# Half 1's Strassen products ahead of its plain output tile, and two sums of the cross pairs in halves

## The chip, the cores and the metric

The kernel runs on one core of a Trainium2 chip. The metric is the device time of one execution in microseconds; the median over several runs counts. Engines in the profile's names: PE is TensorE's matmuls, PEld its weight loads, DVE is VectorE, ACT is ScalarE, POOL is GpSimd, SP is SyncE, which issues DMAs.

## What is computed

Attention with a local window (96 positions) and a few global keys (8), over 4 batches of 8 heads, 768 positions and head size 64, followed by a gated feed-forward layer on the 3072 x 512 result. Cut to what matters here:

```python
x = attention(q, k, v)                       # 3072 x 512
gate = np.maximum(x @ w_gate, 0.0)           # 3072 x 1536
val  = x @ w_val                             # 3072 x 1536
out  = (gate * val) @ w_out                  # 3072 x 512, float32
```

## The kernel before

**Halves and stages.** The 3072 rows are worked on in eight *halves* c = 0 to 7 (half a batch each, 384 rows, three tiles n of 128 rows). In the steady part, the attention of half c + 1 runs in between the feed-forward work of half c. Halves 0 and 1 share one stage, called stage 1 here: first the gate and value products of both, then the output tiles of both, with the attention of half 2 in between. From half 2 on each half is a stage.

**Feed-forward of a half (`ffn_pieces`).** `f1` holds 24 pieces: for each of 12 column blocks fc a gate product (four matmuls of 384 columns, line 607; ReLU on ScalarE, line 614) and a value product (four matmuls, line 607; the multiplication with the gate on VectorE, line 620, into `ht`). Their results lie in a PSUM pool `ff` of three banks, handed out in turn: a gate takes the bank that the value product two blocks earlier left, a value product the bank of the gate one block earlier. `f2` holds the output pieces. A plain tile (`outp`) is four parts of three matmuls of 512 columns (line 627) into one `ff` bank, a copy on ScalarE (line 632) and a store on SP's queue (line 633).

**Strassen products (`winograd`).** Two output tiles are made together with seven products instead of eight, m1 to m7, six matmuls of 256 columns each (line 549), in an order given as a tuple; in half 1 it is m1, m5, m4, m6, m2, m3, m7. They need four sums of `ht` blocks, s1 to s4 (`add`, line 535, on VectorE, over six blocks or, with two indices, over some of them), and four sums of blocks of the output weights, t1 to t4 (`wo_sum`, line 835, made once, in two parts each, during stage 1). m1 (copy at line 566), m6 (copy at 584) and m7 (additions at 588 and 589) build up in one `ff` bank "a"; m5 (copy at 581) and m3 (addition at 574) in another, "b"; m4 (copy at 578) and m2 (addition at 569) each have a bank of the attention's pool `x`. The copies are ScalarE's, the additions VectorE's. m6 and m7 add onto what is already in bank a, so m7 cannot start before m6's copy has read the bank.

Half 1 has three tiles: n = 0 and 1 as a Strassen pair, n = 2 plain. Halves 4 to 7 have no plain tile: their third tiles are paired across halves (4 with 5, 6 with 7). The seven products of such a cross pair are made in half 5 and half 7; their sums come from `add3`, a second `add`.

**Where the sums stand.** `behind[fc]` lists sums that are issued on VectorE right after the multiplication of block fc (`val_and_sums`). `rest` is the tuple of the sums that need the last blocks; they are inserted between output pieces.

**The order of the work.** The order on each engine is the program's order, written out by hand. `weave` walks through the feed-forward pieces, adds up their weights (0.65 for each) and issues an attention piece, or another placed item, as soon as the walked share of the total reaches the item's place. `spread(items, first, last)` gives a list of items evenly spaced places. So stage 1 reads:

```python
weave(f1_0[G[2]] + f1_1[G[2]] + f2_0 + f2_1,
      [(0.33, order_k[2]), (0.38, order_k[3])],
      spread(attention_pieces(2), 0.375, 0.925), spread(early_pieces(3), 0.58, 0.88),
      spread([... wo_sum(j, part) ... for j in (1, 3, 2, 4) for part in range(2)], 0.1, 0.74))
```

**Attention of a half.** It is made in four pairs of heads, p = 0 to 3. For a pair: scores in two groups of two banks of the pool `x` (line 397), Exp on ScalarE (line 406), masks on VectorE (line 359), then one sum with the values for each of the two heads (line 427, one `x` bank each), Ln and Exp on ScalarE (lines 436, 441), and the normalisation on VectorE into `xT` (line 446), which the next half's gate and value products read. The pool `x` has five banks, handed out in turn in program order to scores, sums, m4 and m2 alike.

Of the kernel before, what the change touches and what calls it, by code (L numbers as in the profile page):

```python
# [15 lines left out]
def kernel(  # L16
# [83 lines left out]
    def w_of(t, dc, fc):  # L100
        f = fc % GW
        return t[fc // GW][:, dc, f * 128 : (f + 1) * 128]
# [495 lines left out]
    def ffn_pieces(c):  # L598
        ht = ht_pool.tile([128, N_FC, QH], BF16, name="ht")
        st = {}  # L600

        def product(w, key, fc, d0, d1):
            key = key, fc
            if d0 == 0 and key not in st:
                st[key] = psum["ff"].tile([128, 512], FP32, name="ff_ps")
            for dc in range(d0, d1):
                nc.tensor.matmul(st[key][:, 0:QH], lhsT=w_of(w, dc, fc), rhs=xT_of[c][:, dc, :],  # L607
                                 start=(dc == 0), stop=(dc == N_DC - 1))

        def gate(fc, d0=0):  # L610
            product(wg, "g", fc, d0, N_DC)
            psg = st["g", fc]
            gr = gr_pool.tile([128, QH], BF16, name="grelu")
            nc.scalar.activation(gr, psg[:, 0:QH], AF.Relu, bias=0.0, scale=1.0)  # L614
            st["gr", fc] = gr

        def val(fc, d0=0):
            product(wv, "v", fc, d0, N_DC)
            psv = st["v", fc]
            nc.vector.tensor_tensor(ht[:, fc, :], psv[:, 0:QH], st["gr", fc], op=ALU.mult)  # L620

        def outp(n, part):
            if part == 0:
                st["o"] = psum["ff"].tile([128, 512], FP32, name="ff_ps")
            ps2 = st["o"]
            for fc in range(part * N_FC // 4, (part + 1) * N_FC // 4):
                nc.tensor.matmul(ps2, lhsT=ht[:, fc, n * 128 : (n + 1) * 128],  # L627
                                 rhs=wo_sb[:, fc, :],
                                 start=(fc == 0), stop=(fc == N_FC - 1))
            if part == 3:  # L630
                osb = late["osb"].tile([128, DM], FP32, name="osb")
                nc.scalar.copy(osb, ps2)
                nc.sync.dma_start(out=out_v[c, n], in_=osb)

        def begin():
            two = psum["s"].tile([128, 2, 512], FP32, name="s_ps")
            st["g", 1], st["v", 1] = two[:, 0], two[:, 1]
            for d0, d1 in ((0, 2), (2, N_DC - 1)):
                for key, w in (("g", wg), ("v", wv)):
                    for fc in range(2):  # L640
                        product(w, key, fc, d0, d1)

        plain = range(NN) if c < 1 else () if c - c % 2 in PAIRED else (NN - 1,)
        add, products = winograd([(c, ht, 0), (c, ht, 1)], "sums", (1, 5, 6, 4, 7, 2, 3) if c == NHALF - 1 else
                                 (1, 2, 5, 6, 4, 3, 7) if c in PAIRED else (1, 5, 4, 6, 2, 3, 7))
        behind = {2: [lambda: add(3, 0, 3)], 7 if c == 2 else 5: [lambda: add(3, 3, 6)], 8: [lambda: add(1, 0, 3)],
                  9: [lambda: add(2, 0, 3)], 10: [lambda: add(4, 0, 3)]}
        rest = tuple(lambda j=j: add(j, 3, 6) for j in (1, 2, 4))
        if c in PAIRED:
            third_of[c] = ht  # L650
        elif c - 1 in PAIRED:
            add3, products3 = winograd([(c, ht, NN - 1), (c - 1, third_of[c - 1], NN - 1)], "sums3",
                                       (1, 5, 4, 6, 2, 3, 7))
            behind.update({1: [lambda: add3(1)], 6: [lambda: add3(2)], 7: [lambda: add3(3)]})
            rest = (lambda: add3(4),) + rest

        def val_and_sums(fc):
            val(fc)
            for f in behind.get(fc, ()):
                f()  # L660

        begin_of[c] = (begin, lambda fc=0: gate(fc, N_DC - 1), lambda fc=0: val(fc, N_DC - 1))
        f1 = []
        for fc in range(N_FC):
            f1.append((0.65, lambda fc=fc: gate(fc)))
            f1.append((0.65, lambda fc=fc: (val if c < 1 else val_and_sums)(fc)))
        f2 = [(0.65, lambda n=n, part=part: outp(n, part))
              for n in plain for part in range(4)]
        if c >= 1:
            f2 += (products3 if c - 1 in PAIRED else []) + products  # L670
            places = (2, 3, 5) if plain else (0, 1, 2) if c in PAIRED else (0, 1, 2, 3)
            for at, f in list(zip(places, rest))[::-1]:
                f2.insert(at, (0.0, f))
        return f1, f2


    def spread(items, first, last):

        n = len(items)
        return [(first + (i + 0.5) / n * (last - first), f) for i, (_, f) in enumerate(items)]  # L680
# [100 lines left out]

    stack = open_psum(ff=2, s=2, t=2)
    f1_0, f2_0 = ffn_pieces(0)
    f1_1, f2_1 = ffn_pieces(1)
    g_of = [lambda fc=fc: begin_of[0][1](fc) for fc in range(2)] + [f for _, f in f1_0[4::2]]
    v_of = [lambda fc=fc: begin_of[0][2](fc) for fc in range(2)] + [f for _, f in f1_0[5::2]]
# [18 lines left out]
    for f in ("m0 g0 g1 v0 m3 K3 m2 g2 m1 v1 K2 v2 S30 K0 S31 K1 S21 g3 S20 v3 S01 A3 N3 S00 S11 "  # L805
              "g6 g7 A2 S10 g4 v7 A0 N2 v4 v6 A1 N0 N1 g5 v5").split():
        i = int(f[1])
# [20 lines left out]
    def wo_sum(j, part):  # L828
        n2 = N_FC // 2
        i = slice(part * n2 // 2, (part + 1) * n2 // 2)  # L830
        b = lambda upper, cols: wo_sb[:, upper * n2 : (upper + 1) * n2][:, i, cols]
        t = {k: late["t"][k][:, i] for k in late["t"]}
        x, y, op = {1: (b(0, c1), b(0, c0), ALU.subtract), 2: (t[3], b(0, c0), ALU.add),
                    3: (b(1, c1), b(0, c1), ALU.subtract), 4: (t[2], b(1, c0), ALU.subtract)}[j]
        nc.vector.tensor_tensor(t[j], x, y, op=op)
# [9 lines left out]
    for f in (*casts[:7], lambda: nc.gpsimd.tensor_copy(held, wo_sb[0:1, N_FC - 1, 0:1]),  # L845
# [7 lines left out]
          [(0.33, order_k[2]), (0.38, order_k[3])],  # L853
          spread(attention_pieces(2), 0.375, 0.925), spread(early_pieces(3), 0.58, 0.88),
          spread([(0.0, lambda j=j, part=part: wo_sum(j, part)) for j in (1, 3, 2, 4) for part in range(2)],
                 0.1, 0.74))

    ahead = {}
    for c in range(2, NHALF):
        placed = []  # L860
        if c + 2 < NHALF:
            load_qk(c + 2, 0, H)
            load_v_half(c + 2)
            placed.append(spread(early_pieces(c + 2), 0.25, 0.75))
        if c + 1 < NHALF:
            pieces = ahead.pop(c + 1, None) or attention_pieces(c + 1)
            if c in PAIRED:

                placed.append([(0.76, pieces[-2][1]), (0.84, pieces[-1][1])])
                placed.append(spread(pieces[:-2], 0.05, 0.7))  # L870
            else:
                placed.append(spread(pieces, *(0.07, 0.82) if c == 2 else (0.0, 0.8)))
        if c + 1 in PAIRED:
            ahead[c + 2] = attention_pieces(c + 2)
            placed.append(spread([ahead[c + 2].pop(0) for _ in range(3)], *(0.885, 0.975) if c - 1 in PAIRED else (0.82, 0.93)))
        f1, f2 = ffn_pieces(c)
        weave(f1 + f2, *placed)
# [35 lines left out]
```

## Time and profile before

| | |
|---|---|
| median of 3 runs | 239.83 us (239.14 to 240.46) |
| time of the profiled execution | 240.08 us |
| its span on the core | 238.3 us |
| TensorE matmuls busy | 231.7 us (97%), 1977 of them |
| VectorE busy | 171.8 us (72%) |
| ScalarE busy | 156.1 us (66%) |
| GpSimd busy | 89.5 us (38%) |

The profile is of one execution; its rows give start and duration of groups of instructions. A row of TensorE's timeline merges neighbouring matmuls of one kind, and the drawn end of a matmul is a model: groups that follow each other without a wait overlap in the drawing. Starts are therefore compared with starts. Stage 1's output tiles run from about 57 to 76 us, half 2's gate and value products begin at about 76 us, and half 5 runs from about 156 to 185 us. TensorE's listed waits over the whole span add up to 2.9 us, 1.3 of it the first one.

### The profile page before, as it was taken

The numbers are of one execution on the slowest core, as the hardware profiler recorded it, in microseconds if no ns is written. First come the engines' busy times: TensorE is split into PE (matmuls) and PEld (weight loads), VectorE is DVE, ScalarE is ACT, GpSimd is POOL, SyncE is SP. The second block draws the span as 40 slices with busy tenths as digits, with TensorE's granted clock in tenths as the row PEclk, the third lists the DMA queues.
The fourth block names the chain that finished last, engine by engine and source line by source line (L and its number), as shares of the span: only waits on it lengthen the run. The fifth ranks groups of instructions, "written<-read, shape, count | busy, mean of one in ns | idle before, by whom it ended". The sixth has DMA issues, their size and how long they took to land.

```text
span 238.3 us, 5431 instructions
## 1 busy us (share of the span) xinstructions
PE 231.7 (97%) x1977; PEld 150.1 (63%) x1981; DVE 171.8 (72%) x456; ACT 156.1 (66%) x358; POOL 89.5 (38%) x204
## 2 busy tenths in 40 slices
PE   7899999999999999999999999999999999999994
PEld 3655565655557566666667666856588666766683
DVE  7775965768756778666787677868985786955752
ACT  5896983438767777757777678557686578634330
POOL 6795897007433860903275042723350000000000
PEclk9999999999999999999999999999999999999999
DMA  6999999993996897098519955198432200020022
GB/s 208 183 170 174 241 263 213 191 162 47 286 205 124 260 194 135 10 183 259 101 33 111 236 155 111 25 157 249 78 59 88 90 1 0 4 88 0 3 80 97
DMA packets 70515, 31.42 MB, mean 132 GB/s; under 512 B 47176, under 2 KB 67400, under 8 KB 70488
## 3 DMA queue, kind: packets, MB, share of 16 engines
q0 software_dynamic: 32800, 8.71, 36.0%
q1 hardware_dynamic: 36472, 21.45, 34.3%
q10 hardware_dynamic: 1216, 0.92, 1.2%
q8 instruction: 15, 0.25, 0.4%
q14 instruction: 12, 0.10, 0.1%
HBM read 28.41 MB, written 6.29 MB: 146 GB/s over the span
## 4 chain that ended last, share of the span: by engine, by line
PE 86%; DMA 7%; DVE 2%; POOL 1%; ACT 1%; issue 1%; DVEq 0%
PE ff_ps L607 50%; PE ff_ps L549 12%; DMA wg<-in_moe_w_gate_dram 7%; PE ff_ps L627 7%; PE x_ps L427 6%; PE x_ps L549 5%; PE x_ps L397 4%; PE t_ps L700 1%; PE t_ps L459 1%; POOL kq L737 1%; PE t_ps L272 1%; DVE es L359 0%; DVE ht L620 0%; ACT lnd L436 0%; DVE osb L574 0%
## 5 line engine op out<-in xcount | busy, mean ns | idle before, releaser
L607 PE MATMUL ff_ps<-xT,wg 128*128 128x384 bf16 x380 | 77.7, 326 | 0.4 <-DMA wg<-in_moe_w_gate_dram 0.2
L607 PE MATMUL ff_ps<-xT,wv 128*128 128x384 bf16 x380 | 77.6, 326 | 0.2 <-DVE osb L574 0.2
L614 ACT ACTIVATE grelu<-ff_ps 128x384 bf16<-128x384 f32 x95 | 46.5, 491 | 45.1 <-PE ff_ps L607 23.2
L620 DVE TENSOR_TENSOR ht<-ff_ps,grelu 128x384 bf16<-128x384 f32 x95 | 52.7, 555 | 30.2 <-PE ff_ps L607 19.1
L607 PEld LDWEIGHTS <-wg 128*128 128x128 bf16 x384 | 36.1, 98 | 23.6 <-issue 1.0
L607 PEld LDWEIGHTS <-wv 128*128 128x128 bf16 x384 | 35.8, 98 | 23.3 <-issue 0.5
L406 ACT ACTIVATE es<-x_ps 128x360 bf16<-128x360 f32 (+2 forms) x96 | 35.6, 447 | 3.2 <-PE x_ps L397 3.2
L359 DVE TENSOR_TENSOR es<-es,m_all 128x432 bf16<-128x432 bf16 (+4 forms) x108 | 29.7, 325 | 6.0 <-ACT es L406 5.8
L446 DVE TENSOR_TENSOR xT<-x_ps,rcp 64x384 bf16<-64x384 f32 x48 | 26.6, 554 | 9.2 <-ACT rcp L441 8.4
L436 ACT ACTIVATE lnd<-x_ps 64x384 f32<-64x384 f32 x48 | 23.3, 485 | 10.9 <-PE x_ps L427 10.2
L363 POOL CAST kqc<-ks 128x384 bf16<-128x384 f32 x24 | 12.1, 554 | 31.7 <-DMA ks<-in_k_dram 31.7
L549 PEld LDWEIGHTS <-s 128*128 128x128 bf16 x216 | 21.1, 98 | 2.9 <-issue 0.4
L549 PE MATMUL ff_ps<-t,s 128*128 128x256 bf16 x162 | 21.6, 272 | 0.3 <-ACT osb L584 0.3
L427 PE MATMUL x_ps<-es,vbuf 128*128 128x216 bf16 (+4 forms) x216 | 21.8, 225 | 0.0
L137 POOL DMA_DIRECT2D vbuf<-in_v_dram x25 | 21.6, 881 | 0.3 <-DVE s L535 0.3
L427 PEld LDWEIGHTS <-vbuf 128*128 128x128 bf16 x216 | 15.8, 97 | 6.8
L627 PE MATMUL ff_ps<-wo_sb,ht 128*128 128x512 bf16 x68 | 17.6, 379 | 0.2
L549 PEld LDWEIGHTS <-ht 128*128 128x128 bf16 x162 | 15.5, 98 | 2.3
L263 POOL COPY kT<-kqT 128x240 bf16<-128x240 bf16 x16 | 7.1, 442 | 22.2 <-DMA kqT<-kqc 19.2
L363 POOL CAST kqc<-qs 128x384 bf16<-128x384 f32 x24 | 12.1, 541 | 6.2 <-DMA qs<-in_q_dram 6.2
L535 DVE TENSOR_TENSOR s<-ht 128x384 bf16<-128x384 bf16 (+1 forms) x32 | 12.5, 392 | 0.8
L441 ACT ACTIVATE rcp<-lnd 128x384 f32<-128x384 f32 x24 | 12.6, 524 | 0.8
(118 smaller groups left out, 247.0 us busy)
## 6 DMA issues: line engine op xcount, KB each, us to landing
out_dram<-osb SPq DMA_DIRECT2D x23, 256.0 KB, 2.4
ks<-in_k_dram SPq DMA_DIRECT2D x6, 768.0 KB, 6.2
qs<-in_q_dram SPq DMA_DIRECT2D x6, 768.0 KB, 11.5
vbuf<-in_v_dram POOLq DMA_DIRECT2D x21, 120.0 KB, 7.7
wo_sb<-in_moe_w_out_dram POOLq DMA_DIRECT2D x1, 1536.0 KB, 19.0
wg<-in_moe_w_gate_dram POOLq DMA_DIRECT2D x2, 512.0 KB, 9.8
wv<-in_moe_w_val_dram POOLq DMA_DIRECT2D x2, 512.0 KB, 11.0
wg<-in_moe_w_gate_dram POOLq DMA_DIRECT2D x2, 256.0 KB, 5.8
```

Of the source, the lines that this page charges most:

```text
L137: nc.gpsimd.dma_start(out=v_dst(b, NG + r0, NG + r0 + n, j), in_=v[b, :, KT * j + r0 : KT * j + r0 + n, :].rearrange("h p d -> p h d"))
L359: nc.vector.tensor_mul(for_all, for_all, mk)
L363: nc.gpsimd.tensor_copy(kqc[:, :, i].rearrange("t n (h d) -> t h n d", d=D)[:, 2 * p : 2 * p + 2], of[s][:, 2 * p : 2 * p + 2, :].rearrang ...
L406: nc.scalar.activation(es[:, e, 0:c], banks[e][:, 0:c], AF.Exp, bias=0.0, scale=scale)
L427: nc.tensor.matmul(av3[:, :, a : a + w], lhsT=vb[:, j, z0 : z0 + 128], rhs=es[:, e, c : c + NN * w].rearrange("k (n p) -> k n p", n=NN), s ...
L436: nc.scalar.activation(ln[o0 : o0 + 64], av[d0 : d0 + 64, 0:QH], AF.Ln, bias=0.0, scale=1.0)
L446: nc.vector.tensor_tensor(xT_of[s][r, p, :], av_of[s, p, e][r, 0:QH], av_of[s, p, "r"][r], op=ALU.mult)
L549: nc.tensor.matmul(st[key][:, 0:D2], lhsT=left(i), rhs=right(i), start=start and i == 0, stop=i == N2 - 1, skip_group_check=not start)
L607: nc.tensor.matmul(st[key][:, 0:QH], lhsT=w_of(w, dc, fc), rhs=xT_of[c][:, dc, :], start=(dc == 0), stop=(dc == N_DC - 1))
L614: nc.scalar.activation(gr, psg[:, 0:QH], AF.Relu, bias=0.0, scale=1.0)
L620: nc.vector.tensor_tensor(ht[:, fc, :], psv[:, 0:QH], st["gr", fc], op=ALU.mult)
L627: nc.tensor.matmul(ps2, lhsT=ht[:, fc, n * 128 : (n + 1) * 128], rhs=wo_sb[:, fc, :], start=(fc == 0), stop=(fc == N_FC - 1))
```

## The change

Three things are changed.

1. Half 1's seven Strassen products come ahead of its plain tile. Before, the plain tile's four parts came first and the products ended the stage; now the four parts of the plain tile (its quarters) do. The three sums in `rest` (second halves of s1, s2 and s4), which stood between the pieces of half 1's own outputs, are inserted into half 0's output pieces, at places 3, 6 and 9 of its list.
2. The sums s2 and s3 of the cross pairs (halves 5 and 7) are issued in two operations of three blocks each instead of one of six: s2 behind value blocks 3 and 6, s3 behind 4 and 7, where they stood whole behind 6 and 7.
3. The weight sums t1 to t4 are spread over 0.1 to 0.66 of stage 1 instead of 0.1 to 0.74.

```diff
@@ -651,7 +651,9 @@
         elif c - 1 in PAIRED:
             add3, products3 = winograd([(c, ht, NN - 1), (c - 1, third_of[c - 1], NN - 1)], "sums3",
                                        (1, 5, 4, 6, 2, 3, 7))
-            behind.update({1: [lambda: add3(1)], 6: [lambda: add3(2)], 7: [lambda: add3(3)]})
+            behind[1] = [lambda: add3(1)]
+            for fc, j, i in ((3, 2, 0), (4, 3, 0), (6, 2, 3), (7, 3, 3)):
+                behind[fc] = [lambda j=j, i=i: add3(j, i, i + 3)]
             rest = (lambda: add3(4),) + rest
 
         def val_and_sums(fc):
@@ -666,7 +668,12 @@
             f1.append((0.65, lambda fc=fc: (val if c < 1 else val_and_sums)(fc)))
         f2 = [(0.65, lambda n=n, part=part: outp(n, part))
               for n in plain for part in range(4)]
-        if c >= 1:
+        if c == 1:
+
+            f2 = products + f2
+            for at, f in zip((3, 6, 9), rest):
+                f2_0.insert(at, (0.0, f))
+        elif c > 1:
             f2 += (products3 if c - 1 in PAIRED else []) + products
             places = (2, 3, 5) if plain else (0, 1, 2) if c in PAIRED else (0, 1, 2, 3)
             for at, f in list(zip(places, rest))[::-1]:
@@ -853,7 +860,7 @@
           [(0.33, order_k[2]), (0.38, order_k[3])],
           spread(attention_pieces(2), 0.375, 0.925), spread(early_pieces(3), 0.58, 0.88),
           spread([(0.0, lambda j=j, part=part: wo_sum(j, part)) for j in (1, 3, 2, 4) for part in range(2)],
-                 0.1, 0.74))
+                 0.1, 0.66))
```

On TensorE and ScalarE the number of instructions stays the same; VectorE gets four more.

## The prediction

> **What bounds the kernel now.** I read the page's busy times first, then TensorE's waits, then the timelines of TensorE, ScalarE and VectorE around the places where TensorE waits.
>
> ```profile
> PE 231.7 (97%) x1977; PEld 150.1 (63%) x1981; DVE 171.8 (72%) x456; ACT 156.1 (66%) x358; POOL 89.5 (38%) x204
> ...
> PEclk9999999999999999999999999999999999999999
> ```
>
> TensorE is busy 231.7 of 238.3 us at full granted clock. A faster VectorE or ScalarE is worth only what TensorE waits for them.
>
> ```profile
> PE ff_ps L549 <- ACT osb L584: 0.3, 1, 0.3
> PE ff_ps L607 <- DVE osb L574: 0.2, 1, 0.2
> PE ff_ps L607 <- DVE ht L620: 0.2, 1, 0.2
> ```
>
> These are all the waits that the change can touch (the others are start-up). The first two end stage 1, the third is in half 5. The rows give their true size:
>
> ```profile
> 73.87 0.82 PE L549 MATMUL x_ps<-wo_sb,ht 128*128 128x256 bf16 x6
> 74.53 0.82 PE L549 MATMUL ff_ps<-wo_sb,s 128*128 128x256 bf16 x6
> 75.60 0.81 PE L549 MATMUL ff_ps<-t,s 128*128 128x256 bf16 x6 [0.26 <-ACT osb L584]
> 76.25 0.81 PE L607 MATMUL ff_ps<-xT,wg 128*128 128x384 bf16 x4
> 77.31 0.81 PE L607 MATMUL ff_ps<-xT,wv 128*128 128x384 bf16 x4 [0.24 <-DVE osb L574]
> ```
>
> Undisturbed groups start 0.65 us apart (73.87 to 74.53), though each is drawn 0.82 long. m7 starts 1.07 after m3: it lost 0.42. Half 2's first value product starts 1.06 after its gate product: it lost 0.41. A wait's cost here is its listed idle time plus 0.16.
>
> ```profile
> 70.52 0.59 ACT L632 COPY osb<-ff_ps 128x512 f32<-128x512 f32 x1 [0.16 <-PE ff_ps L627]
> 71.01 0.84 ACT L406 ACTIVATE es<-x_ps 128x360 bf16<-128x360 f32 x2
> ...
> 74.77 0.52 ACT L441 ACTIVATE rcp<-lnd 128x384 f32<-128x384 f32 x1
> 75.20 0.35 ACT L584 COPY osb<-ff_ps 128x256 f32<-128x256 f32 x1
> ```
>
> m6, started at 73.22, had ended at 74.03, but its copy (L584) stood behind the attention's Ln and Exp on ScalarE until 75.20; m7 adds onto the bank that this copy reads. In the same way L574 stood behind the last normalisations on VectorE (until 76.52) and held the bank of half 2's value product.
>
> ```profile
> 169.27 0.81 PE L607 MATMUL ff_ps<-xT,wv 128*128 128x384 bf16 x4
> ...
> 170.26 0.81 PE L607 MATMUL ff_ps<-xT,wg 128*128 128x384 bf16 x4 [0.17 <-DVE ht L620]
> ```
>
> ```profile
> 167.04 0.56 DVE L620 TENSOR_TENSOR ht<-ff_ps,grelu 128x384 bf16<-128x384 f32 x1 [0.37 <-PE ff_ps L607]
> 167.52 0.71 DVE L535 TENSOR_TENSOR s<-s,ht 128x768 bf16<-128x768 bf16 x1
> 168.15 1.59 DVE L359 TENSOR_TENSOR es<-es,m_all 128x432 bf16<-128x432 bf16 x4
> 169.66 0.55 DVE L620 TENSOR_TENSOR ht<-ff_ps,grelu 128x384 bf16<-128x384 f32 x1
> ```
>
> In half 5, gate 9 takes the bank that value 7 leaves (three banks in turn); value 7's multiplication waits behind a 768-wide sum and four masks. Gate 9 starts 0.99 after value 8 instead of 0.65: 0.34 lost. All three losses make 1.17 us: the most that can be won.
>
> **Part 1: stage 1's order.** No work is added or taken away; I lay out the new order with the old rows. Up to 66.33 nothing on TensorE changes. Then three matmuls end half 0's last tile (0.65); m1 at 66.98, m5 at 67.64 (its copy is now at once behind m1's on ScalarE), pair 3's scores from 68.3 with their switch (0.47 together), m4 due at 68.77.
>
> The five x banks go round: pair 2's scores X0 to X3, pair 1's sums X4 and X0, pair 3's scores X1 to X4. Next before came pair 2's sums (X0, X1), m4 (X2), pair 3's sums (X3, X4), m2 (X0). Now it is m4 (X0), pair 2's sums (X1, X2), m2 (X3), pair 3's sums (X4, X0). Two waits are new:
> - m4's X0 is free when pair 1's second normalisation ends, 68.74; with the 0.05 between a release and a start (L584's end 75.55, m7 75.60) m4 starts at 68.79: 0.02 lost.
> - m2's X3 holds pair 3's scores of the second group until their Exp has run. That Exp now stands on ScalarE behind m6's copy, and m6's copy behind m6. Pair 2's first sum is at 69.44, m6 at 69.72, the second sum at 70.37, so m2 is due at 70.65. m6 ends 0.81 after its start, 70.53; its copy starts at 70.58. L632 above lasts 0.59 and the next activation starts 0.49 after it, 0.10 before its end; so after a copy of 0.35 the Exp starts at 70.83, and one of the 360-wide ones lasts 0.48: 71.31. m2 starts at 71.36: **0.71 lost**. Behind that Exp wait only its twin and pair 2's second Ln.
>
> The old waits go. m7 comes at 72.67, long after m6's copy (70.93). Half 2's value product takes the bank of m7, whose additions end by 75.4, before 77. What is late next: pair 3's sums at 73.33 (VectorE makes m2's addition 72.22 to 72.65, then two masks to 73.17: in time), the plain tile's 12 matmuls from 73.94 (2.6), gate 0 at 76.54, value 0 at 77.19 against 77.31 before. Gate 0's fourth matmul needs pair 3's normalisation: Ln, Ln, Exp end about 75.3, the normalisations 76.5, needed at 77.08. Sum: -0.83 + 0.73 = **-0.10 us**. Bounds of the new waits: 0 (the bank is free in time) to 1.1 (m2 needs the twin Exp too, 0.36 later); I take 0.73, since every row in it is measured at this shape.
>
> Edits at nothing: the three second-half sums move into half 0's output tiles (0.35 each, 1.05 in all) under 1.37 us in which VectorE idles before 62.68, waiting for an Exp. Without that cover, pair 2's scores at 63.45 would wait for pair 0's normalisation, by up to 1.05 less 0.2 of slack. The wo sums (0.74 to 0.66) come at most 2 us earlier; t4's second half then ends about 65.9 instead of 69.33, before m4. On SP the plain tile's store is now last, issued near 77.4 instead of 77.9 for m7's, so half 4's loads behind it are no later. POOL's queue is the same.
>
> **Part 2: sums in halves.** A 768-wide sum takes 0.55 (546 ns mean), a 384-wide one 0.35, and the next starts about 0.08 before its end. Each split adds some 0.12 to 0.15 us of VectorE, four times. In half 7 TensorE never waits, so it costs nothing. In half 5 the first halves go behind values 3 and 4: at 163.1, in 0.83 us of idle time, and at 164.5, where they push pair 2's normalisations and value 5 (165.72) by 0.17; gate 7 takes that bank at 166.50, and is due at 166.77. Behind value 6 there is 0.27 less work, more at the stretched pace (0.71 for 0.55) that this stretch shows. The masks' inputs are ready by 167.6, so value 7 starts 0.27 to 0.36 earlier, and gate 9 loses 0.07 to 0 instead of 0.34: **-0.29 us**. Bounds: -0.34 to +0.1.
>
> The stretch has a cause in the rows: while POOL's casts run (166.86 to 169.2), the sum takes 0.71 for 0.55, the first two masks 0.68 and 0.48 for 0.37 and 0.18, and two casts 0.83 and 0.65 for 0.51. The new half-sum at 164.5 meets the four casts from 164.55; that is rival 3 below. The Trainium skill, SBUF — State Buffer, Who interferes with whom, says that a VectorE instruction with two SBUF inputs and a GpSimd one that reads SBUF exclude each other, the later one waiting out the earlier. The stretched rows agree. Perfetto Trace Analysis, Optimizing Scalar/DVE Operations, in the Trainium skill puts some 60 ns of access overhead on each VectorE operation on SBUF and advises larger ones when the engine is saturated, smaller ones when it is not but makes others wait. By its first half the four splits would be an estimated 0.24 us of loss.
>
> **Sum.** Against the profiled execution (240.08; span 238.3 and 1.8 around it): -0.10 - 0.29 = -0.39, 239.69. That execution is 0.25 above the median of 239.83, so a median of 239.44: **239.4**.
>
> **Rivals.**
> 1. No new wait: X3 is free when m2 comes. Then all 1.17 comes back: 238.7. For it: every old wait does go. Against: m6's copy stands ahead of that Exp, and m6 ends only 0.12 before m2 is due.
> 2. Slower: half 2's start becomes bound by pair 3's normalisation. m2's addition now stands on VectorE ahead of pair 3's last masks, and m7's two additions (0.75) ahead of pair 3's normalisations. I left 0.58 us. Before, sums to end of normalisation took 3.91 (72.56 to 76.47). If that holds and the 0.75 comes on top, 4.66 stands against 3.75 to gate 0's fourth matmul: 0.91 lost. With no gain in half 5: -0.83 + 0.73 + 0.91 = +0.81, 240.6; with the masks at the stretched pace (1.59 for 0.98) +1.4. It decides once the chain takes over 3.75. Against: ScalarE's copies that lengthened it before are gone from it.
> 3. The change doesn't do what it says in half 5: the half-sum at 164.5 waits out a cast (0.51). Value 5 ends near 167.0, gate 7 starts at 167.05 for 166.77, 0.28 lost, and the win at gate 9 is spent. Left is -0.10: 239.7.
>
> **How the numbers follow.** Forecast 0.50, rival 1 0.15, rival 2 0.20, rival 3 0.15. A difference under 0.5% (1.2 us) is about what a measurement of this kernel can't tell from none; the runs themselves spread over 1.3. The forecast and rival 3 are "same" but for 0.03 on each side by that spread; rival 1, at 1.17, falls over the line half the time (0.07); rival 2, between 0.8 and 1.4, half the time (0.10). Faster 0.10, same 0.77, slower 0.13. The range runs from rival 1 with little spread, 238.6, to rival 2's first price, 240.6.
>
> **What would show it.** Right: no wait at m7 or half 2's value 0; a wait of about 0.55 listed (0.71 start to start) at m2, L549 x_ps, released by ACT es L406; half 2's gate 0 at about 76.5; none or under 0.1 at gate 9. Wrong: a listed wait for DVE xT L446 at half 2's start (rival 2), no wait at m2 (rival 1), one at half 5's gate 7 (rival 3), or any new wait before 66 us.

## The result and the profile after

The changed kernel takes 238.91 us (median of 22 runs, 238.27 to 240.08) against 239.74 for the kernel before in the same sessions (22 runs): ratio 0.9965, interval 0.9953 to 0.9978, so 0.83 us less, between 0.53 and 1.13. The forecast was 239.4, or 0.39 less. Its profiled execution took 238.84 us with a span of 237.0.

TensorE's timeline at the end of stage 1 (start, duration, line, tiles, count):

```profile
66.16 0.81 PE L627 MATMUL ff_ps<-wo_sb,ht 128*128 128x512 bf16 x3
...
70.22 0.44 PE L427 MATMUL x_ps<-es,vbuf 128*128 128x216 bf16 x4
70.50 0.82 PE L549 MATMUL x_ps<-wo_sb,ht 128*128 128x256 bf16 x6
71.15 0.82 PE L549 MATMUL ff_ps<-wo_sb,s 128*128 128x256 bf16 x6
71.81 0.82 PE L549 MATMUL ff_ps<-t,s 128*128 128x256 bf16 x6
72.46 0.71 PE L427 MATMUL x_ps<-es,vbuf 128*128 128x216 bf16 x8
73.01 2.75 PE L627 MATMUL ff_ps<-wo_sb,ht 128*128 128x512 bf16 x12
75.60 0.81 PE L607 MATMUL ff_ps<-xT,wg 128*128 128x384 bf16 x4
76.25 0.81 PE L607 MATMUL ff_ps<-xT,wv 128*128 128x384 bf16 x4
```

No row has a wait. m7 (71.81) follows m3 by 0.66 and half 2's value product follows its gate by 0.65: the two old waits are gone. m2 (70.50) follows pair 2's second sum at once: the new wait of 0.71 us, on which the forecast's wash rested, is not there. From the first of these rows to the last it is 10.09 us; the same two points lie 10.98 apart before (66.33 to 77.31). Stage 1 gives **0.89 us**.

ScalarE's rows around m2 are where the forecast had them, once its times are moved by the 0.17 us that this execution was ahead at 66.16:

```profile
70.42 0.37 ACT L584 COPY osb<-ff_ps 128x256 f32<-128x256 f32 x1
70.69 0.84 ACT L406 ACTIVATE es<-x_ps 128x360 bf16<-128x360 f32 x2
```

m6's copy was forecast for 70.41 and the Exp for 70.66. So m2 started before the Exp that should have freed its bank: it was given another bank.

In half 5, gate 9 follows value 8 by 0.82 us, against 0.99 before and 0.65 undisturbed:

```profile
168.20 0.81 PE L607 MATMUL ff_ps<-xT,wv 128*128 128x384 bf16 x4
169.02 0.81 PE L607 MATMUL ff_ps<-xT,wg 128*128 128x384 bf16 x4
```

That is 0.17 us. The rest of the 1.3 us between the two spans is 0.17 that this execution was already ahead before 28 us, where the change touches nothing, and less than 0.1 elsewhere.

Two theories had to be told apart. **Theory A**: stage 1's new order gives the 0.89, and half 5's 0.17 comes from the halved sums. **Theory B**: half 5's wait depends on when POOL's casts of q run beside VectorE's masks, and the halved sums have little to do with it. And two rivals for stage 1: the order of the products, or VectorE's sums having been moved up.

### The profile page after: what moved, and what is told of

The parts are those of the page before. It is cut to its first block, busy times and chain, and to the rows that moved or that the text cites. A ratio compares the mean times of both kernels' runs of the same rounds, so it can differ in the third digit from the quotient of the medians.

```text
span 237.0 us, 5436 instructions
## 1 busy us (share of the span) xinstructions
PE 231.0 (97%) x1981; PEld 149.5 (63%) x1981; DVE 171.5 (72%) x460; ACT 156.4 (66%) x358; POOL 88.7 (37%) x204
## 4 chain that ended last, share of the span: by engine, by line
PE 87%; DMA 9%; POOL 1%; DVE 1%; issue 0%; SPq 0%
PE ff_ps L607 52%; PE ff_ps L549 12%; DMA wg<-in_moe_w_gate_dram 7%; PE ff_ps L627 7%; PE x_ps L427 6%; PE x_ps L549 5%; PE x_ps L397 4%; DMA kq<-in_k_dram 2%; PE t_ps L459 1%; POOL kq L744 1%; PE s_ps L459 0%; POOL wv L155 0%; POOL wg L155 0%; DVE qk L281 0%; SPq L182 0%
## 5 line engine op out<-in xcount | busy, mean ns | idle before, releaser
L359 DVE TENSOR_TENSOR es<-es,m_all 128x432 bf16<-128x432 bf16 (+4 forms) x108 | 28.6, 316 | 5.1 <-ACT es L406 5.0
L535 DVE TENSOR_TENSOR s<-ht 128x384 bf16<-128x384 bf16 (+1 forms) x34 | 13.1, 386 | 0.8
```

The source lines that it names most:

```text
L359: nc.vector.tensor_mul(for_all, for_all, mk)
```

## The experiments

Each code cut is the edit against the changed kernel, where nothing else is said. Stage 1's length below is from the start of the last three matmuls of half 0's third tile to the start of half 2's first value product.

**Stage 1's edits alone: the order, the moved sums and the earlier weight sums** (called "order alone" below)

```diff
-            behind[1] = [lambda: add3(1)]
-            for fc, j, i in ((3, 2, 0), (4, 3, 0), (6, 2, 3), (7, 3, 3)):
-                behind[fc] = [lambda j=j, i=i: add3(j, i, i + 3)]
+            behind.update({1: [lambda: add3(1)], 6: [lambda: add3(2)], 7: [lambda: add3(3)]})
```

> Half 1's order and the earlier weight sums alone, the cross pairs' sums whole. Theory (stage 1 gives the larger part, because both old waits go and m2's bank is free): from the last three matmuls of half 0's third tile to half 2's first value product 10.1 us as in the changed kernel, against 10.98 before; half 5's gate 9 starts 0.99 us after value 8 as before. In all 0.9 us less than before, ratio 0.996. Rival (the halved sums carry the gain, stage 1 is the wash that the prediction had): ratio 0.999.

Measured: 238.75 us, ratio 0.9964 (0.9948 to 0.9981), the whole gain of the change. Stage 1 takes 10.09 us (66.20 to 76.29). The expectation for half 5 was wrong: with the sums whole, gate 9 waits for nothing.

```profile
168.24 0.81 PE L607 MATMUL ff_ps<-xT,wv 128*128 128x384 bf16 x4
168.89 0.81 PE L607 MATMUL ff_ps<-xT,wg 128*128 128x384 bf16 x4
```

This is the same instruction order in half 5 as before, and 0.34 us less of a wait. Theory A's second half falls: 0.34 us can go without any halved sum.

**The halves alone**

```diff
-            behind.update({1: [lambda: add3(1)], 6: [lambda: add3(2)], 7: [lambda: add3(3)]})
+            behind[1] = [lambda: add3(1)]
+            for fc, j, i in ((3, 2, 0), (4, 3, 0), (6, 2, 3), (7, 3, 3)):
+                behind[fc] = [lambda j=j, i=i: add3(j, i, i + 3)]
```

(the edit against the kernel before)

> The cross pairs' sums in halves alone, stage 1 as before. Theory: stage 1 10.98 us with both waits; gate 9 0.82 us after value 8, as in the changed kernel, 0.17 us won, ratio 0.9993. Rival (the halves carry the gain): 0.6 us or more won, ratio 0.9975 or less.

Measured: 239.49 us, ratio 1.0000 (0.9987 to 1.0013). Stage 1 takes 10.97 us with both waits; gate 9 starts 0.64 after value 8, not the expected 0.82. The halves alone move nothing that can be measured.

**The plain tile first, all else as changed**

```diff
-            f2 = products + f2
+            f2 = f2 + products
```

> The changed kernel, but with half 1's plain tile ahead of its products again; the sums moved into half 0's tiles, the weight sums up to 0.66 and the halved sums stay. Theory (the order of the products carries stage 1's gain): m7 waits 0.42 us start to start for m6's copy and half 2's first value product 0.41 for VectorE, as before; only half 5's 0.17 us are won, ratio 0.9993. Rival (VectorE was late because the sums and weight sums stood among its last pieces): both waits at least halve, stage 1 10.5 us or less, ratio 0.997.

Measured: 239.67 us, ratio 1.0003 (0.9988 to 1.0017). Stage 1 takes 10.97 us, with both waits back:

```profile
76.23 0.81 PE L549 MATMUL ff_ps<-t,s 128*128 128x256 bf16 x6 [0.25 <-ACT osb L584]
76.89 0.81 PE L607 MATMUL ff_ps<-xT,wg 128*128 128x384 bf16 x4
77.93 0.81 PE L607 MATMUL ff_ps<-xT,wv 128*128 128x384 bf16 x4 [0.23 <-DVE osb L574]
```

So without the order of the products nothing is won; moving the sums and the weight sums up brings nothing by itself.

**m2 in the bank that the prediction gave it**

```diff
             V2(r(0, 0), block("c", raw(0, 1), of_b(1, c0)), r(0, 0), op=ALU.add)
+            if pair[0][0] == 1:
+                nc.vector.tensor_copy(rc_pool.tile([1, 1], BF16, name="held2"), st["d"][0:1, 0:1])
```

> The changed kernel, with m4's bank kept by a one-element copy on VectorE after m2's addition, so that m2 gets the bank of pair 3's second group of scores, the one that the prediction gave it. Theory (the prediction's price was right and only the bank wrong): m2 waits 0.55 us as listed, 0.7 start to start, for ACT es L406; stage 1 10.8 us; 0.7 us slower than the changed kernel, ratio to before 0.9985. Rival (the price was wrong too, the Exp comes in time): no wait at m2, ratio 0.9955.

Measured: 239.47 us, ratio 0.9992 (0.9975 to 1.0010). Stage 1 takes 10.81 us (65.97 to 76.78), and m2 waits as it was forecast to:

```profile
70.03 0.43 PE L427 MATMUL x_ps<-es,vbuf 128*128 128x216 bf16 x4
71.03 0.81 PE L549 MATMUL x_ps<-wo_sb,ht 128*128 128x256 bf16 x6 [0.56 <-ACT es L406]
```

It starts 1.00 after the second sum instead of 0.28: 0.72 us, against the 0.71 of the prediction's working. The price was right; the bank was not. The built programs, in which every tile has its bank, show why. The banks of pool `x` are not handed out in turn, as the description ahead of the prediction has it: each new tile gets the bank whose last reader comes first in the program. For stage 1's tiles of the kernel before, both rules give the same banks, so that order could not tell them apart. In the changed kernel m4's copy, which frees m4's bank, stands ahead of the Exps of pair 3's second group, and m4 and m2 have one and the same bank. It was free from 69.87 (69.50 + 0.37) on:

```profile
69.50 0.37 ACT L578 COPY osb<-x_ps 128x256 f32<-128x256 f32 x1 [0.27 <-PE x_ps L549]
```

In this run a late reader keeps m4's bank, and m2 has the bank that the group's first Exp frees.

**The weight sums as late as before**

```diff
-                 0.1, 0.66))
+                 0.1, 0.74))
```

> The changed kernel with the weight sums spread to 0.74 again. On VectorE the second half of t4 then stands behind pair 1's normalisations, which end 0.1 us before m4 is due. Theory (the earlier weight sums are needed by the new order): m4 starts about 0.5 us late, a wait of some 0.35 us listed there for DVE t; ratio to before 0.9975. Rival (they are not needed): stage 1 10.1 us, no new wait, ratio 0.9955.

Measured: 238.93 us, ratio 0.9964 (0.9936 to 0.9991), too wide to tell 0.25 us. In the profile stage 1 takes 10.32 us: the fourth matmul of m4 starts about 0.25 late (at 69.80), since the half of t4 that it needs ends only at 69.75 (69.19 + 0.56). The first three matmuls need the other half, which the expectation of 0.5 forgot. So in this one profile the shift to 0.66 is worth about a quarter of a microsecond to the new order; the times neither confirm nor deny it.

**Half 5: other places for the sums or the casts**

```diff
-            for fc, j, i in ((3, 2, 0), (4, 3, 0), (6, 2, 3), (7, 3, 3)):
-                behind[fc] = [lambda j=j, i=i: add3(j, i, i + 3)]
+            for fc, j, i in ((3, 2, 0), (3, 3, 0), (7, 2, 3), (8, 3, 3)):
+                behind[fc] = behind.get(fc, []) + [lambda j=j, i=i: add3(j, i, i + 3)]
```

> The changed kernel with the cross pairs' half-sums in other places: both first halves behind value 3, the second halves behind 7 and 8, so that none stands between value 6 and the masks. Theory (value 7 is late by what stands ahead of it on VectorE): gate 9 starts 0.65 us after value 8, 0.17 us less than the changed kernel, ratio to before 0.995. Rival (the work is only pushed on): another gate or value product of half 5 waits by 0.1 us or more, nothing won.

```diff
-            placed.append(spread(early_pieces(c + 2), 0.25, 0.75))
+            placed.append(spread(early_pieces(c + 2), *(0.45, 0.85) if c == 5 else (0.25, 0.75)))
```

> The changed kernel with half 7's casts on POOL, which run in half 5 while the sums and masks do, spread from 0.45 to 0.85 of that half instead of 0.25 to 0.75. Theory (what is left of gate 9's delay comes from VectorE's operations stretching beside POOL's casts): the half-sums ahead of value 7 take 0.35 us instead of 0.6, the four masks 0.98 instead of 1.28, gate 9 starts 0.65 us after value 8; 0.17 us less than the changed kernel, ratio 0.995. Rival (VectorE's queue is too long there in any case): gate 9 still 0.75 us or more after value 8.

Measured: 238.69 us, ratio 0.9952 (0.9926 to 0.9977), and 238.53 us, ratio 0.9940 (0.9916 to 0.9964). Gate 9 follows value 8 by 0.65 in both. But so it did in the run with whole sums, so neither tells what it was meant to tell; nor do their times, whose intervals overlap that of the changed kernel (0.9953 to 0.9978). The second one did not even move the casts: POOL's casts of q still started when the load of q had landed, which was 0.34 us before value 6 started on TensorE.

That number is what orders the profiles. "Casts" is the start of the four casts of q on POOL less the start of value 6 on TensorE; "gate 9" is its start less that of value 8.

| kernel | sums | casts | gate 9 |
|---|---|---|---|
| before | whole | +0.75 | 0.99 |
| changed, first profile | halves | +0.52 | 0.82 |
| order alone | whole | -0.09 | 0.65 |
| m2's bank | halves | -0.19 | 0.64 |
| halves alone | halves | -0.38 | 0.64 |
| plain tile first | halves | -0.59 | 0.64 |
| weight sums at 0.74 | halves | -0.71 | 0.65 |

In this table only the two profiles with a late start of the casts have a late gate 9, whatever the sums.

**The casts held back.** To set this start by the program instead of leaving it to the load, a one-element copy on POOL, which reads value 6's block, was put ahead of the four casts, with the sums whole, in halves, and in the other places:

```diff
             val(fc)
+            if c == 5 and fc == 7:
+                nc.gpsimd.tensor_copy(rc_pool.tile([1, 1], BF16, name="gate"), ht[0:1, 6, 0:1])
```

> Half 1's new order with the cross pairs' sums whole, and the four casts of half 7's q on POOL held until value 6 of half 5 is multiplied, by a one-element copy ahead of them. Theory (gate 9's wait comes from these casts running beside VectorE's sum and masks, and so from when the q load lands): masks stretch to 1.3 us or more together, value 7's multiplication is late, gate 9 starts 0.85 to 1.05 us after value 8 instead of 0.65. Rival (the wait has another cause): 0.65 as in the run with the order alone.

> The changed kernel (sums in halves) with the same held casts. Theory (halving takes 0.27 us from what stands ahead of value 7, which only shows when the casts are late): gate 9 starts 0.2 to 0.3 us earlier than with whole sums, 0.65 to 0.8 after value 8. Rival (halving brings nothing even then, since a half-sum waits out a cast as a whole one does): the same as with whole sums within 0.1 us.

> The half-sums in other places (both first halves behind value 3, the second ones behind 7 and 8) with the same held casts. Theory: no sum stands between value 6 and the masks, value 7 is another 0.3 us earlier, gate 9 starts 0.65 us after value 8. Rival (the casts meet the masks whatever stands ahead of them): 0.75 or more.

With whole sums, VectorE's, POOL's and TensorE's rows read:

```profile
166.48 0.55 DVE L535 TENSOR_TENSOR s<-s,ht 128x768 bf16<-128x768 bf16 x1
166.95 2.75 DVE L359 TENSOR_TENSOR es<-es,m_all 128x432 bf16<-128x432 bf16 x4
169.62 0.55 DVE L620 TENSOR_TENSOR ht<-ff_ps,grelu 128x384 bf16<-128x384 f32 x1
```

```profile
167.02 1.83 POOL L363 CAST kqc<-qs 128x384 bf16<-128x384 f32 x4
```

```profile
168.23 0.81 PE L607 MATMUL ff_ps<-xT,wv 128*128 128x384 bf16 x4
170.22 0.81 PE L607 MATMUL ff_ps<-xT,wg 128*128 128x384 bf16 x4 [1.17 <-DVE ht L620]
```

The four masks take 2.75 us instead of 0.98; gate 9 follows value 8 by 1.99. With halves it is 1.76 (168.16 to 169.92), with the sums elsewhere 1.52 (168.38 to 169.90). One run each: 240.02, 239.73 and 239.72 us, with 239.45 for the kernel before. The masks stretched to 2.75 in all three, far beyond the expected 1.3, so the absolute numbers missed, and in the third run the rival's number (0.75 or more) came true. The hold put the casts 1.75 to 1.95 us after value 6's start, later than any load did (0.75 at most), so these runs show the cause and not the size of the wait before. The steps between them (0.23 and 0.24) are what moving a half-sum away from ahead of the masks is worth in that case, from one profile each. Theory B holds: the wait is the casts', and the halves shorten it only when the casts are late.

**The casts past the masks, and the changed kernel again**

```diff
             val(fc)
+            if c == 5 and fc == 7:
+                nc.gpsimd.tensor_copy(rc_pool.tile([1, 1], BF16, name="gate"), ht[0:1, 7, 0:1])
```

> The changed kernel with half 5's q casts held until value 7 is multiplied, past the masks. Theory (casts cost only where they meet masks ahead of a product that TensorE waits for): the four masks take 0.98 us, gate 9 starts 0.65 us after value 8 in any run, and no later product of half 5 waits; as fast as the changed kernel's best executions, up to 0.2 us below its median, ratio to before 0.9955. Rival (the collision only moves): gate 10 or a later product waits by 0.2 us or more, ratio 0.997 or above.

> The changed kernel itself once more, beside the run with the held casts. Theory: stage 1 10.1 us as in its first profile; gate 9 between 0.65 and 0.85 us after value 8, by how late the q casts begin after value 6 starts on TensorE (0.17 us lost for 0.52, nothing for a start before it). Rival (halving the sums fixed what gate 9 loses): always 0.82.

Measured: 238.65 us, ratio 0.9961 (0.9943 to 0.9979), and 238.74 us, ratio 0.9961 (0.9943 to 0.9980). With the casts held until value 7 the masks take 0.98 and gate 9 comes at 0.65; no other product of half 5 waits. The changed kernel's second profile has its casts 0.64 before value 6, and gate 9 at 0.65 as well, with the same code as in its first profile, where it was 0.82. POOL's rows of the two, the first profile's first:

```profile
165.56 2.10 POOL L363 CAST kqc<-qs 128x384 bf16<-128x384 f32 x4 [0.32 <-DMA qs<-in_q_dram]
```

```profile
163.85 1.98 POOL L363 CAST kqc<-qs 128x384 bf16<-128x384 f32 x4 [0.23 <-DMA qs<-in_q_dram]
```

Value 6 started at 165.04 and at 164.49, and both times the casts had waited for the load of q. In these medians nothing is left to be won by holding the casts.

## Why the prediction was right or wrong

**What bounds the kernel: right.** The only listed waits that could be won were those three, and the difference between the two profiles lies there and at the start. The loss per wait, listed idle time plus 0.16, held within 0.01 in every run (0.56 listed and 0.72 lost at m2). One row was misread without harm: before, the last normalisations on VectorE ended at 76.47 (75.33 + 1.14), not 76.52, and m2's addition stood between them and L574; the loss of 0.41 is as stated.

**The old waits of stage 1 go: right**, both, and the run with the plain tile first shows that they stay without the new order. The term (0.83) was a little small: m6 also waited 0.11 before, for m1's copy behind ScalarE's Ln and Exp (L566, 72.81 to 73.16). That is too short to be listed; it shows when pair 3's two sums to the next product (72.56 to 73.22, 0.66) are compared with the 0.55 that they take now.

**m2's new wait of 0.71: wrong.** The step that failed is "the five x banks go round". Every duration in its sum came out within 0.03 us, but the bank was another one. What the runs showed in its place is that m2 gets the bank that m4's copy has freed, and waits for nothing; given the other bank, it does lose the 0.72. No wait at m2 is the prediction's own sign of being wrong, and rival 1 came true for stage 1: 0.89 won instead of 0.10. m4's wait for its bank was there, about 0.05 instead of 0.02.

**Half 5's 0.29: wrong as a gain of the change.** The row of 1.59 us of masks beside POOL's casts was read rightly as a stretch, but the stretch was taken as a property of the kernel rather than of the one execution. Whether the casts run then depends on when q's load lands. In the changed kernel's first profile gate 9 still lost 0.17, in its second nothing, and the halves alone give a ratio of 1.0000. Two of its sums were off too. Halving takes 0.20 us from behind value 6 (0.55 less 0.35), not 0.27; the held runs show 0.21 on VectorE from value 6's multiplication to value 7's (3.62 and 3.41). And with the next operation starting 0.08 before the end, a split adds 0.07 (twice 0.27 for 0.47), not 0.12 to 0.15. How often the kernel before has its wait is not known: there is one profile of it. Adding 0.89 for stage 1 and nothing for half 5 agrees with the measured 0.83 (0.53 to 1.13).

**That the time came near the forecast is in part luck.** 239.4 was forecast, within 238.6 to 240.6, and 238.91 measured, but neither term held: stage 1 gave 0.79 more than its 0.10, half 5 none of its 0.29. The second error hid a part of the first, and 0.44 was left between the two medians' differences (0.83 and 0.39).

**Rivals 2 and 3** did not occur. Half 2's first gate product needs pair 3's normalisation, which ended at 75.66 (74.52 + 1.14), 0.4 before its fourth matmul started (75.60 + 0.49). The half-sum at 163.37 did meet a cast (0.60 for 0.35), but gate 7 came on time (165.71, 0.67 after value 6).

**The edits at nothing** cost nothing: before 66 us TensorE has no new wait. The shift of the weight sums, entered as no cost, carries a part of the gain: without it m4 lost about 0.25 in the one profile taken.

## What to carry to other kernels

When a wait's price hangs on which buffer of a pool an operation gets, look up the buffer in the built program before pricing it; here the place of the last reader in the program decided, not the number of the request. A stall that one profile shows beside a transfer's landing time is to be taken as chance until a second profile, or a run that holds the transfer, shows it again. Where TensorE is the bound, work that needs the other engines only at its very end (here a plain tile, with one copy) can fill the time behind work whose results must pass through busy engines on the way (here the products that build up in shared banks); in this kernel that order was worth 0.89 us.

## What the runs showed of the hardware

By the drawn rows, one VectorE mask was held out by four POOL casts in a row. In the run with whole sums and held casts, the first mask alone, two SBUF inputs of 432 elements, took 2145 ns, from 166.95 to 169.10; the other mask of this size in the same run took 0.37 us. Meanwhile the four casts ran undisturbed from 167.02 to 168.85; the mask's drawn start is even 0.07 before the first cast's. The view of line 359 in that stretch (duration min/median/max):

```profile
L359 DVE TENSOR_TENSOR es<-es,m_all x4: 169/332/2145, 166.9 to 169.4; 128x432 bf16<-128x432 bf16 x2, 128x48 bf16<-128x48 bf16 x1, 128x288 bf16<-128x288 bf16 x1
```

The other two held runs show the same: 2149 ns for the first mask with the halved sums, and with the sums elsewhere 1946 ns for the second mask, of 48 elements, which takes 0.17 us otherwise.

The Trainium skill, SBUF — State Buffer, Who interferes with whom, lets the second of two such instructions wait until the first finishes. That agrees for the kind of instruction; here the waiting one was not let in between the first cast and the fourth either. In the profile before, by contrast, the casts stretched as well (0.83 and 0.65 us), so who gives way is not always VectorE; what decides it was not settled.
